# Attention and MoE on one core: PSUM banks and copies of the first two batches rearranged, last output chunk stored in two column halves

## Chip, cores, metric

One core of one Trainium2 chip. The metric is the device time of one execution in microseconds (us); all times below are us. Times inside a profile count from the start of its span, and the span is some 2 us shorter than the execution's time.

## The reference

```python
B, H, S, D = 8, 8, 576, 64; pool = 8; Sp = 72
k_p = k.reshape(B, H, Sp, pool, D).mean(axis=3); v_p = the same of v
attn = softmax(q @ k_p^T / sqrt(D))
x = (attn @ v_p).transpose(0, 2, 1, 3).reshape(4608, 512)
h = x @ w_in                    # 512 -> 2048
out = (h * cos(h)) @ w_out      # 2048 -> 512, fp32
```

## The kernel before

The 4608 tokens are worked in nine tiles of 512. Tile `t` has an up stage (eight blocks of eight 128x512 matmuls into `banks[fp % 3]`, ScalarE's cosine, VectorE's multiply) and a down stage (64 matmuls). The attention of batch `t + 1` is threaded into the down stage of tile `t`. Batch 0 runs alone at the start. Batches 0 and 1 pool k and v and transpose q on TensorE; from batch 2 on, POOL (GpSimd) pools and SP issues DMA transposes of q and of the pooled k. In profiles PE is TensorE, DVE VectorE, ACT ScalarE. `us` are the four units of a batch (256 tokens by four heads), REST its last 64 tokens, S their scores and V their values; `kpz` is the pooled k, `kz` the same transposed, `qT` the transposed q; half clock means that a 128x512 matmul takes 0.43 instead of 0.216. The parts that the argument touches, with cuts marked `...`:

```python
def put_kz(b, ps, pj0, pj1, copies):            # pooled k out of PSUM, four copies
    for a in range(2):
        for r in range(2):
            copies[r](out=dst[half[r], pj0:pj1, a, r, 0:Sp], in_=ps[half[a]])
...
# start, batch 0 ("mixed" = VectorE, ScalarE in turn on one PSUM tile)
q_transpose_mm(0, qbanks, 0, mixed)             # qbanks: two halves of banks[2]
...
pool_k_mm(0, obanks[1], 2, 4, vec2)
warm_up(2, obanks[0])
q_transpose_mm(0, qbanks, 1, vec2)
sums_first(0, us[0], obanks[0])                 # the sums, Ln and Exp(-1) of unit 0
sums_first(0, us[1], obanks[1])
...
# up stage of tile 0, after block 5 and block 6
pool_k_mm(1, obanks[0], 0, 4, mixed)
q_transpose_mm(1, obanks[::-1], 0, mixed_r)
...
# down stage: (number of matmuls before, what is put in)
fill = [(1, REST scores), (4, S 0), (8, REST values), (8, pool_v_mm), (8, S 1), (8, V 0), (16, S 2),
        (16, V 1), (24, S 3), (24, V 2), (36, V 3)]          # tile 0, shortened
...
if 0 < t and b + 1 < B:                          # b = t + 1
    load_kv(b + 1, "k", k); ...; load_kv(b + 1, "v", v)      # POOL's queue
...
if b + 1 < B:
    pool_add(b + 1, "k"); pool_add(b + 1, "v")               # POOL
```

The softmax here doesn't subtract the row's maximum and nothing guards it: scores larger than these inputs give would overflow.

Of the kernel before, what the change touches and what calls it, by code (L numbers as in the profile page):

```python
# [10 lines left out]
BF16 = mybir.dt.bfloat16  # L11
# [3 lines left out]
POOL = 8  # L15
# [4 lines left out]
def kernel(  # L20
# [9 lines left out]
    nc = tc.nc  # L30
    B, H, S, D = q.shape
    Sp = S // POOL
# [51 lines left out]
    def load_even(dst, b, src, j0=0, j1=KCH):  # L84
        nc.gpsimd.dma_start(out=dst[:, j0:j1].rearrange("p j t d -> p j (t d)"), in_=even_view(src, b, j0, j1))
# [36 lines left out]
    def v_part(b):  # L122
        return vz[b % 2][:, :, 0:4:3, :]

    def put_kz(b, ps, pj0, pj1, copies):
        dst = kz[b % 2].rearrange("p (j a r) n -> p j a r n", a=2, r=2)
        for a in range(2):
            for r in range(2):
                copies[r](out=dst[half[r], pj0:pj1, a, r, 0:Sp], in_=ps[half[a]])

    def pool_add(b, which):

# [11 lines left out]
            s = s.rearrange("p (j a) t d -> p j a t d", a=2)  # L144
            add(out=v_part(b), in0=s[..., 0, :], in1=s[..., 1, :], op=ADD)  # L145

    def pool_k_mm(b, bank, pj0, pj1, copies):

        kb = staged["k", b]
        ps = bank[:, 0:(pj1 - pj0) * Sp].rearrange("p (j n) -> p j n", n=Sp)  # L150
        for pj in range(pj0, pj1):
            for t in range(ROW):
                for rows in half:
                    nc.tensor.matmul(ps[rows, pj - pj0, :], lhsT=kb[rows, pj, t, :], rhs=groups[rows, t, :],
                                     start=(t == 0), stop=(t == ROW - 1))
        put_kz(b, ps, pj0, pj1, copies)

    def pool_v_mm(b, pair):
        vb = staged["v", b]
# [16 lines left out]
    def q_flat(b):  # L176
        return staged["q", b].rearrange("p j t d -> p (j t d)")
# [2 lines left out]
        qT_tile(b)  # L180
        nc.sync.dma_start_transpose(out=att["qT", b], in_=q_flat(b))

    def q_transpose_mm(b, banks_, j, copies):

        if ("qT", b) not in att:
            qT_tile(b)
        for bank, g0, g1, copy in zip(banks_, (9 * j, 9 * j + 5), (9 * j + 5, 9 * j + 9), copies):
            ps = bank.bitcast(BF16)[:, 0:(g1 - g0) * 128].rearrange("p (g n) -> p g n", n=128)
            for g in range(g0, g1):
                nc.tensor.matmul(ps[:, g - g0, :], q_flat(b)[:, g * 128:(g + 1) * 128], identity, is_transpose=True)  # L190
            copy(out=att["qT", b][:, g0:g1, :], in_=ps)

    def scores(b, u, pair):
        (c0, n), (h0, nh) = u
# [54 lines left out]
        att["inv", b, u] = inv  # L249

    def values_then(b, u, ao):
        (c0, n), (h0, nh) = u
        ex = att.pop(("ex", b, u))
        for i in range(nh):
            pj, hp = divmod(h0 + i, 2)
            nc.tensor.matmul(ao[hp * 64:hp * 64 + 64, (i // 2) * n:(i // 2 + 1) * n],
                             lhsT=vz[b % 2][:, pj, 3 * hp, :], rhs=ex[:, i * n:(i + 1) * n])
        nc.vector.tensor_mul(out=x_out(b, u, slice(0, 128)), in0=cols(ao, u), in1=cols(att.pop(("inv", b, u)), u))
# [8 lines left out]
    def up_mm(t, fp, k0=0, k1=KCH):  # L267

        h = banks[fp % 3]
        for j in range(2):  # L270
            fc = 2 * fp + j
            for ki in range(k0, k1):
                nc.tensor.matmul(h[:, j, :], lhsT=w_in_sb[fc // 4][:, ki, (fc % 4) * 128:(fc % 4 + 1) * 128],  # L273
                                 rhs=xT[:, ki, t * TILE:(t + 1) * TILE],
                                 start=(ki == 0), stop=(ki == KCH - 1))

    def up_g(t, fp):
        h = banks[fp % 3]
        cos = msb.tile([128, 2, TILE], FP32, name="cos", tag="cos", bufs=2)
        nc.scalar.activation(out=cos, in_=h, func=ACTF.Sin, bias=half_pi[:, :1])  # L280
        nc.vector.tensor_mul(out=g_sb[:, 2 * fp:2 * fp + 2, :], in0=h, in1=cos)  # L281

    def down_mm(o, ms, fc):
        nc.tensor.matmul(o, lhsT=g_sb[:, fc, ms * 128:(ms + 1) * 128],  # L284
                         rhs=w_out_sb[fc // 4][:, fc % 4, :], start=(fc == 0), stop=(fc == FFCH - 1))

    def down_out(t, ms, ps):
        o = msb.tile([128, d_model], FP32, name="o_sb", tag="o_sb")
        nc.vector.tensor_copy(out=o, in_=ps)  # L289
        rows_of = out.rearrange("(b p t) m -> b t p m", b=B, t=ROW)  # L290
        for i, rows in enumerate(half):
            b_, pos = divmod((t * TILE + ms * 128) // 64 + i, ROW)
            nc.sync.dma_start(out=rows_of[b_, ORDER[pos]], in_=o[rows])


    EX = 5
# [43 lines left out]
    load_even(staged["q", 1], 1, q, 2, 4)  # L340
    load_w_out(0)
    load_even(staged["v", 1], 1, v)
    for cg in range(1, 4):
        load_w_out(cg)

    def warm_up(n, bank):

        for i in range(n):
            nc.tensor.matmul(bank, lhsT=warm[:, 0:128], rhs=warm)

    vec2 = (nc.vector.tensor_copy,) * 2
    mixed = (nc.vector.tensor_copy, nc.scalar.copy)
    mixed_r = mixed[::-1]
    qbanks = [banks[2][:, 0, :], banks[2][:, 1, :]]
    us = BY_HEADS

    warm_up(10, obanks[0])
    pool_k_mm(0, obanks[1], 0, 2, mixed)
    warm_up(2, obanks[0])
    q_transpose_mm(0, qbanks, 0, mixed)  # L360
    warm_up(2, obanks[0])
    scores(0, us[0], banks[0])
    scores(0, us[1], banks[1])
    pool_k_mm(0, obanks[1], 2, 4, vec2)
    warm_up(2, obanks[0])
    q_transpose_mm(0, qbanks, 1, vec2)
    sums_first(0, us[0], obanks[0])
    sums_first(0, us[1], obanks[1])
    scores(0, us[2], banks[0])
    scores(0, us[3], banks[1])  # L370
    nc.vector.memset(kz[1], 0.0)
    pool_v_mm(0, banks[2])
    sums_first(0, us[2], obanks[0])
    sums_first(0, us[3], obanks[1])
    values_then(0, us[0], obanks[0])
    values_then(0, us[1], obanks[1])
    nc.vector.memset(vz[1], float(POOL))
    values_then(0, us[2], obanks[0])
    values_then(0, us[3], obanks[1])
    sin_tables()  # L380

    for t in range(NT):
        b = t + 1
        if t == 0:
            for fp in range(2):
                up_mm(t, fp, 0, 2)
        for fp in range(FFCH // 2):
            up_mm(t, fp, 2 if t == 0 and fp < 2 else 0)
            up_g(t, fp)
            if t == 0:  # L390
                if fp == 5:
                    pool_k_mm(1, obanks[0], 0, 4, mixed)
                    q_transpose_mm(1, obanks[::-1], 0, mixed_r)
                elif fp == 6:
                    q_transpose_mm(1, obanks[::-1], 1, mixed)
            elif b < B:
                if fp == 0:
                    q_transpose(b)
                elif fp == 2:
                    k_transpose(b)  # L400
        mms = [(ms, fc) for ms in range(4) for fc in range(FFCH)]
        if t == 0:
            mms = [(ms, fc) for hm in range(2) for cg in range(4) for ms in range(2 * hm, 2 * hm + 2)
                   for fc in range(4 * cg, 4 * cg + 4)]


        def S_(n, bank):
            return lambda: scores(b, us[n], banks[bank])

        def V_(n, bank):  # L410
            return lambda: values(b, us[n], banks[bank])

        fill = []
        if t < B:
            exp_tables()
            fill = [(1, lambda: scores(t, REST, banks[2])), (8 if t == 0 else 12, lambda: values(t, REST, banks[1]))]
        if t == 0:
            fill[1:1] = [(4, S_(0, 0))]
            fill += [(8, lambda: pool_v_mm(1, banks[2])), (8, S_(1, 0)), (8, V_(0, 2)), (16, S_(2, 0)), (16, V_(1, 1)),
                     (24, S_(3, 0)), (24, V_(2, 2)), (36, V_(3, 1))]  # L420
        elif b < B:
            us = BY_TOKENS
            fill[1:1] = [(5, S_(0, 0))]
            fill += [(15, S_(1, 2)), (18, V_(0, 0)), (25, S_(2, 2)), (28, V_(1, 1)), (35, S_(3, 2)), (38, V_(2, 0)),
                     (46, V_(3, 1))]
        if 0 < t and b + 1 < B:
            load_kv(b + 1, "k", k)
            q_tile(b + 1)
            load_even(staged["q", b + 1], b + 1, q)
            load_kv(b + 1, "v", v)  # L430
        fi = 0
        for n, (ms, fc) in enumerate(mms):
            while fi < len(fill) and fill[fi][0] <= n:
                fill[fi][1]()
                fi += 1
            down_mm(obanks[ms % 2], ms, fc)
            if fc == FFCH - 1:
                down_out(t, ms, obanks[ms % 2])
        if t < B:
            sin_tables()  # L440
        if t == 0:
            load_kv(2, "k", k)
            q_tile(2)
            load_even(staged["q", 2], 2, q)
            load_kv(2, "v", v)
            for i in range(2):
                nc.gpsimd.memset(kpz[i], 0.0)  # L447
        if b + 1 < B:
            pool_add(b + 1, "k")
            pool_add(b + 1, "v")  # L450
# [1 line left out]
_INS = ['q', 'k', 'v', 'moe_w_in', 'moe_w_out']  # L452
_OUTS = [((4608, 512), 'float32')]
# [25 lines left out]
```

## Time and profile before

| quantity | before |
|---|---|
| time, median of the runs beside the changed kernel | 332.41 (331.54 to 332.8) |
| span of the profiled run | 329.6 |
| TensorE (PE) busy | 303.3 (92%) |
| tile 0 up, from the start of the first up matmul to the first down matmul | 22.19 to 43.96 |
| tile 0 down, to the first up matmul of tile 1 | 43.96 to 70.79 |
| tile 1; tile 2 | 39.4; 31.65 |
| end of PE's work to end of span | 4.8 |

A row of the table is a stretch between two starts in the timeline of PE. A steady tile takes 31.65, so whatever is above this is a hole or a lowered clock. Lines from the page, the chain of work, the waits and the timeline are in the prediction. Here is one view that it uses but does not show, the queue of SP (start, duration of the issue, what):

```profile
75.34 8.35 SPq L181 DMA_TRANSPOSE qT<-q_b  x1
83.80 5.40 SPq L168 DMA_TRANSPOSE kz<-kpz  x1
...
113.17 2.82 SPq L181 DMA_TRANSPOSE qT<-q_b  x1
116.08 1.36 SPq L168 DMA_TRANSPOSE kz<-kpz  x1
```

The first pair belongs to tile 1 and stands among POOL's loads (issued at 70.2 to 72.7, landed by 88.9). The second, in tile 2, comes when the last of its loads lands (113.3).

### The profile page before, as it was taken

The page shows a single profiled execution, that of the slowest core. Times are in us where ns is not written, and L with a number is a line of the kernel's source. Part 1 is how long each engine was busy: PE and PEld are TensorE (multiplying, and loading weights), DVE is VectorE, ACT ScalarE, POOL GpSimd, SP SyncE. Part 2 cuts the span into 40 slices and gives each one's busy share as a digit, 9 for nine tenths or more (in the row PEclk, how much of TensorE's full clock was granted, in tenths as well). Part 3 has the DMA queues.
Part 4 walks back from the last instruction along what each step waited for, and adds up shares of the span by engine and source line. Part 5 has one row for each costly group of instructions (what it writes and reads, how often), then busy time and mean ns, then how long its engine had stood idle before and what let it go on. Part 6 is the DMA issues. An engine that isn't in the chain of part 4 may idle for free.

```text
span 329.6 us, 4548 instructions
## 1 busy us (share of the span) xinstructions
PE 303.3 (92%) x1784; PEld 153.4 (47%) x1784; DVE 172.1 (52%) x209; ACT 206.2 (63%) x253; POOL 131.0 (40%) x88
## 2 busy tenths in 40 slices
PE   6769698699499999999999999999999999999994
PEld 2524354344245446544654555456445544444441
DVE  5345433437415574567466647564665556525721
ACT  2566385546549569956994797579668966704500
POOL 8422009983892974395449445931000000000000
PEclk9979897999969999999999999999999999999999
DMA  7999995139909951993299249901290130041032
GB/s 102 188 207 206 207 174 75 33 60 194 171 2 154 212 89 10 178 215 55 29 195 198 35 54 203 187 15 32 47 162 0 33 82 16 2 91 37 0 67 64
DMA packets 47686, 33.60 MB, mean 102 GB/s; under 512 B 25904, under 2 KB 43056, under 8 KB 47664
## 3 DMA queue, kind: packets, MB, share of 16 engines
q0 software_dynamic: 20016, 18.36, 36.3%
q1 hardware_dynamic: 27648, 14.95, 22.5%
q8 instruction: 14, 0.23, 0.3%
q14 instruction: 8, 0.07, 0.1%
HBM read 36.70 MB, written 9.44 MB: 140 GB/s over the span
## 4 chain that ended last, share of the span: by engine, by line
PE 77%; POOL 8%; DMA 6%; ACT 4%; issue 2%; DVE 1%; POOLq 0%; DVEq 0%; ACTq 0%
PE bank L273 34%; PE obank L284 33%; PE bank L199 4%; PE bank L225 4%; POOL kv_st L138 4%; DMA kv_st<-in_k_dram 3%; DMA kz<-kpz 2%; POOL kv_st L139 2%; DMA q_b<-in_q_dram 2%; POOL kpz L447 1%; ACT cos L280 1%; ACT ex L203 1%; ACT L261 1%; POOL kpz L142 1%; ACT lnc L247 1%
## 5 line engine op out<-in xcount | busy, mean ns | idle before, releaser
L284 PE MATMUL obank<-w_out_sb,g_sb 128*128 128x512 bf16 x576 | 140.3, 385 | 3.2 <-DVE o_sb L289 3.2
L273 PE MATMUL bank<-xT,w_in_sb 128*128 128x512 bf16 x576 | 129.0, 385 | 0.0
L280 ACT ACTIVATE cos<-bank,half_pi 128x1024 f32<-128x1024 f32 x72 | 80.2, 1115 | 73.8 <-PE bank L273 73.8
L281 DVE TENSOR_TENSOR g_sb<-bank,cos 128x1024 bf16<-128x1024 f32 x72 | 88.1, 1224 | 55.2 <-ACT cos L280 55.2
L273 PEld LDWEIGHTS <-w_in_sb 128*128 128x128 bf16 x576 | 56.8, 99 | 69.6 <-issue 3.8
L284 PEld LDWEIGHTS <-g_sb 128*128 128x128 bf16 x576 | 56.0, 99 | 58.0 <-issue 6.2
L234 DVE TENSOR_TENSOR xT<-bank,inv 64x512 bf16<-64x512 f32 (+1 forms) x72 | 45.3, 629 | 66.1 <-ACT inv L232 64.0
L138 POOL TENSOR_TENSOR kv_st<-kv_st 72x2048 f32<-72x2048 bf16 x12 | 48.7, 4061 | 32.6 <-DMA kv_st<-in_k_dram 31.9
L231 ACT ACTIVATE lnc<-bank 64x512 f32<-64x512 f32 (+1 forms) x72 | 39.2, 544 | 11.6 <-PE bank L225 9.8
L203 ACT ACTIVATE ex<-bank 72x1024 bf16<-72x1024 f32 (+1 forms) x40 | 36.3, 927 | 7.3 <-PE bank L199 7.2
L289 DVE COPY o_sb<-obank 128x512 f32<-128x512 f32 x36 | 24.2, 689 | 19.0 <-PE obank L284 18.4
L139 POOL TENSOR_TENSOR kv_st<-kv_st 72x1024 f32<-72x1024 f32 x12 | 28.2, 2348 | 1.0
L199 PE MATMUL bank<-qT,kz 128*72 128x256 bf16 (+1 forms) x192 | 23.5, 254 | 5.2 <-DMA kz<-kpz 5.2
L199 PEld LDWEIGHTS <-kz 128*72 128x72 bf16 x192 | 17.9, 117 | 14.5 <-DMA kz<-kpz 5.6
L225 PE MATMUL bank<-ex,vz 72*128 72x256 bf16 (+1 forms) x176 | 20.3, 246 | 2.7 <-DVE vz L164 1.7
L232 ACT ACTIVATE inv<-lnc 128x512 f32<-128x512 f32 (+1 forms) x36 | 21.0, 582 | 1.1
L225 PEld LDWEIGHTS <-vz 72*128 72x128 bf16 x176 | 14.1, 100 | 12.2 <-DVE vz L164 2.0
L145 POOL TENSOR_TENSOR vz<-kv_st 72x512 bf16<-72x512 f32 x6 | 7.6, 1264 | 25.3 <-PE bank L225 24.7
L142 POOL TENSOR_TENSOR kpz<-kv_st 72x512 bf16<-72x512 f32 x12 | 15.0, 1267 | 0.5
L104 POOL DMA_DIRECT2D kv_st<-in_v_dram x6 | 5.0, 841 | 18.9 <-PE bank L162 18.9
L261 ACT ACT_TABLE_LOAD x9 | 11.5, 1283 | 0.9 <-PEq L463 0.7
L264 ACT ACT_TABLE_LOAD x9 | 11.5, 1283 | 0.2
(48 smaller groups left out, 77.7 us busy)
## 6 DMA issues: line engine op xcount, KB each, us to landing
out_dram<-o_sb SPq DMA_DIRECT2D x72, 128.0 KB, 2.7
kv_st<-in_v_dram POOLq DMA_DIRECT2D x8, 576.0 KB, 14.8
kv_st<-in_k_dram POOLq DMA_DIRECT2D x7, 576.0 KB, 8.9
q_b<-in_q_dram POOLq DMA_DIRECT2D x6, 576.0 KB, 11.4
w_in_sb<-in_moe_w_in_dram POOLq DMA_DIRECT2D x4, 512.0 KB, 13.6
w_out_sb<-in_moe_w_out_dram POOLq DMA_DIRECT2D x4, 512.0 KB, 18.5
q_b<-in_q_dram POOLq DMA_DIRECT2D x4, 288.0 KB, 12.2
kv_st<-in_k_dram POOLq DMA_DIRECT2D x2, 288.0 KB, 5.0
```

The source lines that it names most:

```text
L138: add(out=s, in0=x[:, :, 0:4, :], in1=x[:, :, 4:8, :], op=ADD)
L139: add(out=s[:, :, 0:2, :], in0=s[:, :, 0:2, :], in1=s[:, :, 2:4, :], op=ADD)
L199: nc.tensor.matmul(flat[:Sp, i * n:(i + 1) * n].rearrange("p (g n) -> p g n", n=64), lhsT=kz[b % 2][:, 2 * (h0 + i) + r, 0:Sp], rhs=att["q ...
L203: nc.scalar.activation(out=ex[:, 0:nh * n], in_=flat[:Sp, 0:nh * n], func=ACTF.Exp, scale=scale / POOL)
L225: nc.tensor.matmul(pair[:, hp, (i // 2) * n:(i // 2 + 1) * n], lhsT=vz[b % 2][:, pj, 2 * hp:2 * hp + 2, :].rearrange("p a d -> p (a d)"), ...
L231: nc.scalar.activation(out=lnc[half[1 - hp]], in_=pair[half[1 - hp], hp, 0:w], func=ACTF.Ln)
L234: nc.vector.tensor_mul(out=x_out(b, u, half[hp]), in0=cols(pair[half[hp], hp, :], u), in1=cols(inv[half[1 - hp]], u))
L273: nc.tensor.matmul(h[:, j, :], lhsT=w_in_sb[fc // 4][:, ki, (fc % 4) * 128:(fc % 4 + 1) * 128], rhs=xT[:, ki, t * TILE:(t + 1) * TILE], st ...
L280: nc.scalar.activation(out=cos, in_=h, func=ACTF.Sin, bias=half_pi[:, :1])
L281: nc.vector.tensor_mul(out=g_sb[:, 2 * fp:2 * fp + 2, :], in0=h, in1=cos)
L284: nc.tensor.matmul(o, lhsT=g_sb[:, fc, ms * 128:(ms + 1) * 128], rhs=w_out_sb[fc // 4][:, fc % 4, :], start=(fc == 0), stop=(fc == FFCH - 1))
L289: nc.vector.tensor_copy(out=o, in_=ps)
```

## The change

The intent: no two engines on one PSUM tile in the first two batches, so that nobody takes turns; the inverse of each unit made as soon as its sums are there; the down stage of tile 0 in an order in which each bank is free when it is wanted; and a shorter end. The diff, cut to its core:

```diff
-def put_kz(b, ps, pj0, pj1, copies):      # copies[r](...)
+def put_kz(b, ps, pj0, pj1, copy):        # copy(...): one engine
     # pool_k_mm and q_transpose_mm now return a function that takes the copy; q_transpose_mm fills one bank
 # start
-    q_transpose_mm(0, qbanks, 0, mixed)
+    puts = q_transpose_mm(0, banks[2][:, 0, :], 0, 5), q_transpose_mm(0, obanks[0], 5, 9)
+    puts[0](vec)
+    puts[1](act)
 ...
-    warm_up(2, obanks[0])
-    q_transpose_mm(0, qbanks, 1, vec2)
-    sums_first(0, us[0], obanks[0])
+    sums_first(0, us[0], banks[0][:, 0, :])
+    puts = q_transpose_mm(0, banks[2][:, 0, :], 9, 14), q_transpose_mm(0, obanks[0], 14, 18)
+    puts[0](vec)
+    puts[1](act)
 ...  # sums and values of units 2 and 3 likewise in tiles of their own
 # up stage of tile 0: blocks 4 to 6, ScalarE's copy between cosine and multiply
+                if fp == 4:
+                    puts = pool_k_mm(1, obanks[0], 0, 2), pool_k_mm(1, obanks[1], 2, 4)
+                elif fp in (5, 6):
+                    puts = q_transpose_mm(1, obanks[0], g0, g0 + 5), q_transpose_mm(1, obanks[1], g0 + 5, g0 + 9)
+                puts[0](vec)
+                between = ((puts[1], act),)
+            up_g(t, fp, between)
 # down stage of tile 0, shortened
+            (1, REST scores), (2, S 0), (4, pool_v_mm), (8, REST values), (8, S 1), (8, V 0), (14, S 2),
+            (16, V 1), (22, S 3), (32, V 2), (40, V 3)
 # the memsets of kpz go from behind the load of v for batch 2 to the start
 # the last 128 rows
+    def last_chunk():
+        for hc in range(2):
+            ... 16 matmuls of 256 columns into banks[hc]
+            down_out(t, ms, ps, hc * 256, (nc.sync, nc.scalar))
```

More of the change, by code (lines that the diff above doesn't have):

```diff
@@ L128, in put_kz @@
             for r in range(2):
-                copies[r](out=dst[half[r], pj0:pj1, a, r, 0:Sp], in_=ps[half[a]])
+                copy(out=dst[half[r], pj0:pj1, a, r, 0:Sp], in_=ps[half[a]])
     def pool_add(b, which):
@@ L145, in pool_add, with pool_k_mm @@
             add(out=v_part(b), in0=s[..., 0, :], in1=s[..., 1, :], op=ADD)
-    def pool_k_mm(b, bank, pj0, pj1, copies):
+    def pool_k_mm(b, bank, pj0, pj1):
         kb = staged["k", b]
@@ L155, in pool_k_mm @@
                                      start=(t == 0), stop=(t == ROW - 1))
-        put_kz(b, ps, pj0, pj1, copies)
+        return lambda copy: put_kz(b, ps, pj0, pj1, copy)
     def pool_v_mm(b, pair):
@@ L181, in q_transpose, with q_transpose_mm @@
         nc.sync.dma_start_transpose(out=att["qT", b], in_=q_flat(b))
-    def q_transpose_mm(b, banks_, j, copies):
+    def q_transpose_mm(b, bank, g0, g1):
         if ("qT", b) not in att:
             qT_tile(b)
-        for bank, g0, g1, copy in zip(banks_, (9 * j, 9 * j + 5), (9 * j + 5, 9 * j + 9), copies):
-            ps = bank.bitcast(BF16)[:, 0:(g1 - g0) * 128].rearrange("p (g n) -> p g n", n=128)
-            for g in range(g0, g1):
-                nc.tensor.matmul(ps[:, g - g0, :], q_flat(b)[:, g * 128:(g + 1) * 128], identity, is_transpose=True)
-            copy(out=att["qT", b][:, g0:g1, :], in_=ps)
+        ps = bank.bitcast(BF16)[:, 0:(g1 - g0) * 128].rearrange("p (g n) -> p g n", n=128)
+        for g in range(g0, g1):
+            nc.tensor.matmul(ps[:, g - g0, :], q_flat(b)[:, g * 128:(g + 1) * 128], identity, is_transpose=True)
+        return lambda copy: copy(out=att["qT", b][:, g0:g1, :], in_=ps)
     def scores(b, u, pair):
@@ L275, in up_mm, with up_g @@
                                  start=(ki == 0), stop=(ki == KCH - 1))
-    def up_g(t, fp):
+    def up_g(t, fp, between=()):
         h = banks[fp % 3]
@@ L280, in up_g @@
         nc.scalar.activation(out=cos, in_=h, func=ACTF.Sin, bias=half_pi[:, :1])
+        for put, copy in between:
+            put(copy)
         nc.vector.tensor_mul(out=g_sb[:, 2 * fp:2 * fp + 2, :], in0=h, in1=cos)
@@ L285, in down_mm, with down_out @@
                          rhs=w_out_sb[fc // 4][:, fc % 4, :], start=(fc == 0), stop=(fc == FFCH - 1))
-    def down_out(t, ms, ps):
+    def down_out(t, ms, ps, c0=0, queues=(nc.sync, nc.sync)):
         o = msb.tile([128, d_model], FP32, name="o_sb", tag="o_sb")
-        nc.vector.tensor_copy(out=o, in_=ps)
+        n = ps.shape[1]
+        nc.vector.tensor_copy(out=o[:, 0:n], in_=ps)
         rows_of = out.rearrange("(b p t) m -> b t p m", b=B, t=ROW)
@@ L292, in down_out @@
             b_, pos = divmod((t * TILE + ms * 128) // 64 + i, ROW)
-            nc.sync.dma_start(out=rows_of[b_, ORDER[pos]], in_=o[rows])
+            queues[i].dma_start(out=rows_of[b_, ORDER[pos], :, c0:c0 + n], in_=o[rows, 0:n])
+    def last_chunk():
+        t, ms = NT - 1, 3
+        for hc in range(2):
+            ps = banks[hc][:, 0, 0:256]
+            for fc in range(FFCH):
+                nc.tensor.matmul(ps, lhsT=g_sb[:, fc, ms * 128:(ms + 1) * 128],
+                                 rhs=w_out_sb[fc // 4][:, fc % 4, hc * 256:(hc + 1) * 256],
+                                 start=(fc == 0), stop=(fc == FFCH - 1))
+            down_out(t, ms, ps, hc * 256, (nc.sync, nc.scalar))
     EX = 5
@@ L342 @@
     load_even(staged["v", 1], 1, v)
+    for i in range(2):
+        nc.gpsimd.memset(kpz[i], 0.0)
     for cg in range(1, 4):
@@ L349, in warm_up @@
             nc.tensor.matmul(bank, lhsT=warm[:, 0:128], rhs=warm)
-    vec2 = (nc.vector.tensor_copy,) * 2
-    mixed = (nc.vector.tensor_copy, nc.scalar.copy)
-    mixed_r = mixed[::-1]
-    qbanks = [banks[2][:, 0, :], banks[2][:, 1, :]]
+    vec, act = nc.vector.tensor_copy, nc.scalar.copy
     us = BY_HEADS
     warm_up(10, obanks[0])
-    pool_k_mm(0, obanks[1], 0, 2, mixed)
-    warm_up(2, obanks[0])
-    q_transpose_mm(0, qbanks, 0, mixed)
-    warm_up(2, obanks[0])
+    pool_k_mm(0, obanks[1], 0, 2)(vec)
+    warm_up(2, banks[1][:, 0, :])
+    puts = q_transpose_mm(0, banks[2][:, 0, :], 0, 5), q_transpose_mm(0, obanks[0], 5, 9)
+    puts[0](vec)
+    puts[1](act)
+    warm_up(2, banks[1][:, 0, :])
     scores(0, us[0], banks[0])
     scores(0, us[1], banks[1])
-    pool_k_mm(0, obanks[1], 2, 4, vec2)
-    warm_up(2, obanks[0])
-    q_transpose_mm(0, qbanks, 1, vec2)
-    sums_first(0, us[0], obanks[0])
+    pool_k_mm(0, obanks[1], 2, 4)(vec)
+    sums_first(0, us[0], banks[0][:, 0, :])
+    puts = q_transpose_mm(0, banks[2][:, 0, :], 9, 14), q_transpose_mm(0, obanks[0], 14, 18)
+    puts[0](vec)
+    puts[1](act)
     sums_first(0, us[1], obanks[1])
     scores(0, us[2], banks[0])
-    scores(0, us[3], banks[1])
+    scores(0, us[3], banks[2])
     nc.vector.memset(kz[1], 0.0)
-    pool_v_mm(0, banks[2])
+    nc.vector.memset(vz[1], float(POOL))
+    pool_v_mm(0, banks[1])
     sums_first(0, us[2], obanks[0])
-    sums_first(0, us[3], obanks[1])
-    values_then(0, us[0], obanks[0])
-    values_then(0, us[1], obanks[1])
-    nc.vector.memset(vz[1], float(POOL))
-    values_then(0, us[2], obanks[0])
-    values_then(0, us[3], obanks[1])
+    values_then(0, us[0], obanks[1])
+    values_then(0, us[1], banks[1][:, 0, :])
+    sums_first(0, us[3], banks[2][:, 0, :])
+    values_then(0, us[2], obanks[1])
+    values_then(0, us[3], obanks[0])
+    up_mm(0, 0, 0, 2)
+    up_mm(0, 1, 0, 2)
     sin_tables()
@@ L383 @@
         b = t + 1
-        if t == 0:
-            for fp in range(2):
-                up_mm(t, fp, 0, 2)
         for fp in range(FFCH // 2):
             up_mm(t, fp, 2 if t == 0 and fp < 2 else 0)
-            up_g(t, fp)
+            between = ()
             if t == 0:
-                if fp == 5:
-                    pool_k_mm(1, obanks[0], 0, 4, mixed)
-                    q_transpose_mm(1, obanks[::-1], 0, mixed_r)
-                elif fp == 6:
-                    q_transpose_mm(1, obanks[::-1], 1, mixed)
-            elif b < B:
+                if fp == 4:
+                    puts = pool_k_mm(1, obanks[0], 0, 2), pool_k_mm(1, obanks[1], 2, 4)
+                elif fp in (5, 6):
+                    g0 = 9 * (fp - 5)
+                    puts = q_transpose_mm(1, obanks[0], g0, g0 + 5), q_transpose_mm(1, obanks[1], g0 + 5, g0 + 9)
+                if fp in (4, 5, 6):
+                    puts[0](vec)
+                    between = ((puts[1], act),)
+            up_g(t, fp, between)
+            if 0 < t and b < B:
                 if fp == 0:
@@ L415 @@
             exp_tables()
-            fill = [(1, lambda: scores(t, REST, banks[2])), (8 if t == 0 else 12, lambda: values(t, REST, banks[1]))]
+            fill = [(1, lambda: scores(t, REST, banks[2])), (12, lambda: values(t, REST, banks[1]))]
         if t == 0:
-            fill[1:1] = [(4, S_(0, 0))]
-            fill += [(8, lambda: pool_v_mm(1, banks[2])), (8, S_(1, 0)), (8, V_(0, 2)), (16, S_(2, 0)), (16, V_(1, 1)),
-                     (24, S_(3, 0)), (24, V_(2, 2)), (36, V_(3, 1))]
+            fill[1:] = [(2, S_(0, 0)), (4, lambda: pool_v_mm(1, banks[1])), (8, lambda: values(t, REST, banks[2])),
+                        (8, S_(1, 0)), (8, V_(0, 1)), (14, S_(2, 2)), (16, V_(1, 0)), (22, S_(3, 1)), (32, V_(2, 2)),
+                        (40, V_(3, 0))]
         elif b < B:
@@ L431 @@
         fi = 0
+        if t == NT - 1:
+            mms = mms[:-FFCH]
         for n, (ms, fc) in enumerate(mms):
@@ L445 @@
             load_kv(2, "v", v)
-            for i in range(2):
-                nc.gpsimd.memset(kpz[i], 0.0)
         if b + 1 < B:
@@ L450 @@
             pool_add(b + 1, "v")
+    last_chunk()
 _INS = ['q', 'k', 'v', 'moe_w_in', 'moe_w_out']
```

## The prediction

> **What bounds the kernel now.** I read the page first, for the bound of the whole and where it is not kept. Units are us, times count from the span's start.
>
> ```profile
> PE 303.3 (92%) x1784; PEld 153.4 (47%) x1784; DVE 172.1 (52%) x209; ACT 206.2 (63%) x253; POOL 131.0 (40%) x88
> ...
> PE   6769698699499999999999999999999999999994
> ...
> PEclk9979897999969999999999999999999999999999
> ```
>
> TensorE is the bound, but its holes and its lowered clocks lie in the first 12 slices (8.24 us each) and in the last. From there on it is full. The chain of work, in order of time, gives the length of an undisturbed tile of 512 tokens:
>
> ```profile
> 110.39 13.81 PE bank L273 x64
> ...
> 142.03 13.81 PE bank L273 x64
> ...
> 173.68 13.81 PE bank L273 x64
> ```
>
> So a steady tile takes 31.65. Tile 1 started at 70.79 (the timeline of PE), so it took 39.6, which is 7.95 too long. What comes before 70.79 is the part that the change rewrites. The waits of PE name the holes:
>
> ```profile
> PE bank L199 <- DMA kz<-kpz: 5.2, 1, 5.2
> PE obank L284 <- DVE o_sb L289: 3.2, 1, 3.2
> PE obank L190 <- ACT kz L129: 2.5, 1, 2.5
> PE obank L243 <- ACT ex L203: 1.7, 2, 1.2
> PE bank L190 <- DVE qT L191: 1.7, 2, 1.1
> PE bank L225 <- DVE vz L164: 1.7, 1, 1.7
> ```
>
> The first is in tile 1, the second and sixth in the down stage of tile 0, the third in its up stage, the others in the start. The timeline of PE shows that a hole costs more than itself:
>
> ```profile
> 38.10 0.45 PE L190 MATMUL obank<-identity,q_b 128*128 128x128 bf16 x4 [2.49 <-ACT kz L129]
> 38.34 3.55 PE L273 MATMUL bank<-xT,w_in_sb 128*128 128x512 bf16 x8
> ```
>
> Eight matmuls take 3.4 here and 1.73 (8 x 0.216) in a steady tile: half the clock, some 1.6 lost. After the 5.2 hole, and after the 1.7 one at 51.06, it is the same.
>
> **What the Trainium skill says.** "TensorE: Matmul & The Clock Gate", Part 1, says that the clock falls to half after an idle window of about 3.4 us and comes back after a busy one, with a window that runs free. The trace agrees (3.4 against 1.73), though here holes of 1.7 and 2.5 in sparse work were enough. "PSUM — Partial Sum Buffer", section on PSUM bank collisions, says that two engines must not touch one bank and quadrant at once, so accesses must be ordered by bank. The trace agrees with such an order: at L129 VectorE and ScalarE take turns on one tile (36.27 DVE, 36.74 ACT, 37.16 DVE, 37.66 ACT), and PE waits for the last. "Trainium Kernel Development and Optimization", Key Constraints, says that the DMAs of SP, ACT and POOL share 16 DMA engines, so that a second queue saves only issue time. The trace agrees for the sharing: beside the loads of 70 to 89 the transposes of tile 1 took 14.7 and 7.4 to land, and in tile 2 4.8 and 3.8.
>
> **The change, part by part.** I walked the new order of instructions by hand with the old durations.
>
> Start (before: up stage from 22.25). The q transposes of a half go to two tiles, so the second four need not wait for the copy of the first five: scores 0.6 earlier. The Ln and Exp of unit 0 come before the second q half, which lands at 11.8 (issue 4.80 plus 7.0) in both kernels. In the chain of before, ScalarE ran without a pause from 14.16:
>
> ```profile
> 14.16 0.61 ACT lnc L247
> ...
> 14.79 0.64 ACT inv L248
> ...
> 15.45 0.61 ACT lnc L247
> ...
> 16.08 0.63 ACT inv L248
> 16.71 1.42 ACT ex L203 x2
> ```
>
> Now the first pair runs at about 11.6 to 12.8. One q copy comes to ScalarE (0.59), and the last inverse ends near 19.2 instead of 21.0. The first up matmuls need only units 0 and 1, whose values now lie in tiles of their own and are multiplied by 18.4, once the v load (14.6) has been pooled and copied. Up starts at 18.5: **3.7 gained**. All weights are there (the first w_in lands at 17.2, the third at 22.2).
>
> Up of tile 0 (before 22.25 to 43.96, 21.7). Work is 64 x 0.216 = 13.8, k pooling 1.4, transposes 1.65: 16.9. The copies go to VectorE before its multiply (4 x 0.31 or 0.49) and to ScalarE after its cosine (4 x 0.27 or 0.6), each on its own bank, with a whole block of eight matmuls (1.73) before the bank is wanted. So the 2.5 hole and the half clock after it go. I leave 1.5 for the half clock at its start, since the start stays sparse: 18.4, **3.3 gained**, ending at 36.9. k1 (25.1), q1 (30.6), w_in 3 (29.0) and the first w_out (33.0) have landed when wanted.
>
> Down of tile 0 (before 43.96 to 70.79, 26.8). Matmuls 13.8; four scores and four values at 0.44 each, v pooling 1.1, the two small ones 0.5: 18.9. Walking the order leaves three waits: v pooling on the multiply of the last up block, 1.0; the last scores on a values bank, 0.7; the third output row on the copy of the first, 0.5. That is 21.2 with small gaps, no half clock: **5.6 gained**. Tile 1 starts at about 58.2, not 70.8.
>
> Tile 1. The POOL chain moves less. The kpz memsets (3.56) leave it, but k2 lands only at 47.6, behind a full DMA, so the k sums start at 47.6, not 53.5, and the loads for batch 3 go out at 64.3, not 70.2. The transposes of batch 2 go out at about 60.5, ahead of those loads. The 5.2 wait and the half clock after it vanish: **7.95 gained**.
>
> Tile 2. The same collision comes back here. POOL needs 26.9 from loads to loads (70.23 to 97.11), so the loads for batch 4 start near 90.2, and tile 2 starts at 58.2 + 31.65 = 89.8; its transposes go out 2.7 later, into those loads. Before, with loads 0.6 ahead of the tile, kz landed 20.4 after its start and was wanted after 15.2. With two fewer stores in the way I take 19: wait 4, half clock 2: **6 lost**. Tile 3 is then clear of it.
>
> End. The last two lines of the timeline's outputs:
>
> ```profile
> 321.37 0.69 DVE L289 COPY o_sb<-obank 128x512 f32<-128x512 f32 x1 [2.76 <-PE obank L284]
> 324.82 0.69 DVE L289 COPY o_sb<-obank 128x512 f32<-128x512 f32 x1 [2.76 <-PE obank L284]
> ```
>
> From the end of PE's work 4.8 pass. The half-width copy should take about 0.42 (0.27 less, an estimate from 0.69), and two stores issued side by side save one issue of 0.62. The 32 half matmuls cost as much as 16 (0.11 each, as in the scores): **0.9 gained**.
>
> Sum: 3.7 + 3.3 + 5.6 + 7.95 - 6 + 0.9 = 15.45, and 332.6 - 15.45 = **317**.
>
> **Rivals.** (a) The collision does not come back: POOL's loads slip 3 late or more and the transposes pass ahead of them. Then about 311. Against it: each tile POOL gains only 31.65 - 26.9 = 4.75 on PE, so it must pass through the bad zone, about as wide, at some tile. (b) It comes back in full, twice, or the gain before tile 1 is swallowed: the DMA is full up to 46 whatever PE does, so a faster PE only meets later loads. If all of the gain of the first two parts is lost in waits for loads, 324. For it: DMA at 9 tenths in every early slice; against it: by the landing times every load has over 2 to spare. But this also bounds me from the other side: if PE is 3 slower than I think, tile 2 waits that much less. (c) The longer list of VectorE and ScalarE work in up blocks 4 to 6 becomes the bound: 1.23 + 1.26 on VectorE and 1.11 + 1.1 on ScalarE against 1.73 + 1.4 of PE in block 4; it fits, and a miss costs 1. (d) Only the end matters and the rest hides: 331. Nothing in the chain of work, which is PE nearly throughout, speaks for it.
>
> **Range and chances.** Half clock comes by windows that I can't place (each 1.5 to 2), and the collision is between 0 and 8. I take 311 to 323. Under 2% needs more than 326, that is over half of the sum failing: 0.04 for same, 0.01 for slower.
>
> **What would show it.** In the changed profile: the first long L273 block at 18 to 19.5 (the start); no wait for the kz copies over 0.5 (up); down of tile 0 at 21 to 22.5 and no wait for o_sb over 1; no wait for the kz transposes in tile 1 and one of 2 to 6 in tile 2 with matmuls at half clock behind it; the last stores landing about 4 after PE's end. The prediction is wrong if PE waits for w_in or w_out, if tile 1 still waits for kz, or if the collision is seen nowhere.

## The result

| | before | after |
|---|---|---|
| time, median | 332.41 | 318.67 (316.8 to 325.31, 4 runs) |
| ratio | | 0.9572 (0.9519 to 0.9624) |
| profiled span | 329.6 | 316.3 |

The profiled runs and all runs compared here are fast ones; the changed kernel's run of 325.31 counts as slow and is left out. A ratio here is the mean time of one kernel's fast runs over that of the other's of the same rounds, so not quite the ratio of the medians.

The slow runs here need not be a state of the chip. Two were profiled, and in both the time lies in waits of the kernel itself: after_memback waits 13.9 for kz, and ag_whole2q begins its up stage at 21.37 behind a 1.6 wait for v, with 18.4 for the stage where after_gate takes 16.2. Of the 13 runs of the three kernels that meet the collision in tile 2 (the changed one, after_memback, after_warm) four were slow, of the 22 of the gated change two. The run of 325.31 was not profiled; if it is a long wait for kz, the ratio leaves out a part of what the change costs.

Stage by stage, from the timelines of PE of the two profiled runs:

| stretch | before | after | gained | predicted |
|---|---|---|---|---|
| start (first up matmul) | 22.19 | 20.10 | 2.1 | 3.7 |
| tile 0 up | 21.8 | 16.2 | 5.5 | 3.3 |
| tile 0 down | 26.8 | 21.4 | 5.45 | 5.6 |
| tile 1 | 39.4 | 31.6 | 7.8 | 7.95 |
| tile 2 | 31.65 | 40.2 | -8.5 | -6 |
| end, with the half matmuls | | | 0.95 | 0.9 |
| sum | | | 13.3 | 15.45 |

The page of the changed kernel (busy us and share; busy tenths in 40 slices of 7.9 us; granted clock in tenths):

```profile
PE 297.4 (94%) x1766; PEld 154.0 (49%) x1798; DVE 173.3 (55%) x213; ACT 205.7 (65%) x254; POOL 130.9 (41%) x88
...
PE   7789899999999299999999999999999999999995
...
PEclk9799999999999879999999999999999999999999
```

The holes of slices 3 to 12 are gone, and there is one new one in slice 14, with a lowered clock behind it. The waits of PE (total, times, longest):

```profile
PE bank L198 <- DMA kz<-kpz: 6.4, 1, 6.4
PE bank L189 <- DMA q_b<-in_q_dram: 1.9, 1, 1.9
...
PE bank L162 <- DVE g_sb L283: 0.9, 1, 0.9
PE bank L198 <- DVE xT L233: 0.5, 1, 0.5
```

Of the waits before, only that for kz is left at size, and the timeline of PE shows that it now lies in tile 2 (start, duration, what; in brackets the idle time before):

```profile
103.67 1.03 PE L286 MATMUL obank<-w_out_sb,g_sb 128*128 128x512 bf16 x4
111.05 1.07 PE L198 MATMUL bank<-qT,kz 128*72 128x256 bf16 x4 [6.35 <-DMA kz<-kpz]
111.91 3.19 PE L286 MATMUL obank<-w_out_sb,g_sb 128*128 128x512 bf16 x7
```

Seven matmuls took 2.98 to the next start (114.89 less 111.91; 0.43 each) where a steady tile has 1.51. The queues of SP and of POOL show why kz came late:

```profile
61.32 2.90 SPq L181 DMA_TRANSPOSE qT<-q_b  x1
64.33 1.36 SPq L168 DMA_TRANSPOSE kz<-kpz  x1
...
92.31 10.76 SPq L181 DMA_TRANSPOSE qT<-q_b  x1
103.16 5.37 SPq L168 DMA_TRANSPOSE kz<-kpz  x1
```

```profile
80.91 2.49 POOL L142 TENSOR_TENSOR kpz<-kv_st 72x512 bf16<-72x512 f32 x2
...
91.15 0.84 POOL L104 DMA_DIRECT2D kv_st<-in_k_dram  x1
```

The first pair (tile 1) went out before POOL's loads of 65.3 and landed after 4.9 and 3.9. The second (tile 2) went out 1.2 after the first of the next loads, which POOL's queue began at 91.15; qT took 17.8 to land and kz 7.8. The pooled k itself had been ready since 83.4 (the timeline of POOL), so POOL's sums were not what it waited for. In the six collisions looked at (tile 1 before, tile 2 here and in before_early, after_memback and after_warm, tile 3 in after_early) kz landed 0.5 to 4.1 after the last of the three loads, that of v: here at 111.0, v at 108.9.

### The profile page after: what moved, and what is told of

Same layout as the page of the kernel before. It is cut to its first block, busy times and chain, and to the rows that moved or that the text cites. A ratio compares the mean times of both kernels' runs of the same rounds, so it can differ in the third digit from the quotient of the medians.

```text
span 316.3 us, 4555 instructions
## 1 busy us (share of the span) xinstructions
PE 297.4 (94%) x1766; PEld 154.0 (49%) x1798; DVE 173.3 (55%) x213; ACT 205.7 (65%) x254; POOL 130.9 (41%) x88
## 4 chain that ended last, share of the span: by engine, by line
PE 65%; DMA 15%; POOL 11%; ACT 2%; issue 1%; DVE 1%; POOLq 0%; ACTq 0%; DVEq 0%
PE obank L286 29%; PE bank L273 28%; DMA kv_st<-in_k_dram 12%; POOL kv_st L138 6%; PE bank L224 3%; PE bank L198 3%; POOL kv_st L139 3%; DMA kz<-kpz 2%; POOL kpz L142 2%; PE bank L304 1%; ACT ex L202 1%; ACT L261 0%; ACT cos L280 0%; PE obank L256 0%; POOL vz L145 0%
## 5 line engine op out<-in xcount | busy, mean ns | idle before, releaser
L286 PE MATMUL obank<-w_out_sb,g_sb 128*128 128x512 bf16 x542 | 133.1, 382 | 1.1 <-DVE o_sb L292 0.3
L273 PE MATMUL bank<-xT,w_in_sb 128*128 128x512 bf16 x563 | 125.5, 379 | 0.6
L273 PEld LDWEIGHTS <-w_in_sb 128*128 128x128 bf16 x576 | 56.1, 98 | 67.3 <-issue 0.4
L286 PEld LDWEIGHTS <-g_sb 128*128 128x128 bf16 x560 | 54.1, 98 | 52.1 <-issue 2.0
L292 DVE COPY o_sb<-obank 128x512 f32<-128x512 f32 x35 | 23.5, 689 | 15.4 <-PE obank L286 14.8
L224 PE MATMUL bank<-ex,vz 72*128 72x256 bf16 (+1 forms) x176 | 20.1, 244 | 0.3 <-ACT ex L202 0.2
## 6 DMA issues: line engine op xcount, KB each, us to landing
w_out_sb<-in_moe_w_out_dram POOLq DMA_DIRECT2D x4, 512.0 KB, 18.3
```

What stands on the lines that cost most here:

```text
L224: nc.tensor.matmul(pair[:, hp, (i // 2) * n:(i // 2 + 1) * n], lhsT=vz[b % 2][:, pj, 2 * hp:2 * hp + 2, :].rearrange("p a d -> p (a d)"), ...
L273: nc.tensor.matmul(h[:, j, :], lhsT=w_in_sb[fc // 4][:, ki, (fc % 4) * 128:(fc % 4 + 1) * 128], rhs=xT[:, ki, t * TILE:(t + 1) * TILE], st ...
L286: nc.tensor.matmul(o, lhsT=g_sb[:, fc, ms * 128:(ms + 1) * 128], rhs=w_out_sb[fc // 4][:, fc % 4, :], start=(fc == 0), stop=(fc == FFCH - 1))
L292: nc.vector.tensor_copy(out=o[:, 0:n], in_=ps)
```

## Experiments

Each kernel ran beside the kernel before on the same chip; "ratio" is that to the kernel before. "Gate" below means the tiny copy of experiment 2. None gives a wrong result. The runs of experiment 4 are from chip 8, those of the other experiments from chip 11.

**1. after_early and before_early: the transposes issued earlier.**

```diff
-                if fp == 0: q_transpose(b)
-                elif fp == 2: k_transpose(b)
 # in the down stage
+            if n == 36 and b + 1 < B:
+                ...                      # tile 0: the loads of batch 2, moved up with it
+                pool_add(b + 1, "k"); pool_add(b + 1, "v")
+                q_transpose(b + 1); k_transpose(b + 1)
```

> The changed kernel, with the transposes of q and k of batch t+2 issued in the down stage of tile t, ahead of its last two rows of stores, and so ahead of the loads for the next batch; nothing else moves. Theory A (the wait for kz in tile 2 is a collision of the transposes with the loads on the shared DMA engines): the wait of 6.35 us and the half clock after it (about 2.1) go, 318.2 - 8.4 = about 310 us, no wait of PE for kz anywhere. Rival B (the pooled k itself is late, so POOL's chain sets it): the wait stays, 316 to 319. Rival C (the collision only moves to another tile): a wait for kz in tile 3 or later, 314 to 318.

The edit moves POOL's sums (and the loads of batch 2) up in the program with the transposes, as the cut shows, so "nothing else moves" is not exact; their order on POOL's queue stays.

Measured: 317.12 (ratio 0.9588). Theory A's number failed, rival C held. There is no wait in tile 2; in tile 3 PE waits 6.6 for kz. The chain of work of this run names its cause (start, duration, what):

```profile
115.45 8.88 DMA kv_st<-in_k_dram
...
124.81 16.38 DMA kz<-kpz
141.19 0.04 issue
141.23 1.07 PE bank L198 x4
```

The transposes of tile 3's batch were issued at 115.79, POOL's loads at 115.45: moving the transposes by a part of a tile met the next loads, since POOL goes from loads to loads in 26.5 (88.97 to 115.45) while PE takes 31.65. The collision moved, it did not go.

> The kernel before, with the same move of the transposes. Theory A: the 5.2 us wait in tile 1 and the half clock behind it go, 332.4 - 7.95 = about 324.5 us, so the change's other parts are worth the same with and without the collision (after_early about 14 below before_early). Rival B: no change, 331 to 333.

Measured: 324.11 (ratio 0.9794, 0.9737 to 0.9852, unclear at 2%), near theory A's number, and no wait of PE for kz. Against the 331.01 of the same rounds it is 6.9 less; the wait and its half clock are 7.8 in the profile. The transposes of tile 1's batch were issued from 65.07 and landed after 5.1 and 3.7, the loads came at 70.95. The next pair did meet loads (those were issued at 96.4 and after; qT took 14.3 to land, kz 7.4). But its kz landed at 116.4, and tile 2, which starts at 103.33, asks for it 15.2 later, at 118.5: the same collision, hidden.

**2. after_gate: the loads held back behind the transposes.**

```diff
         if 0 < t and b + 1 < B:
+            nc.gpsimd.tensor_copy(out=token, in_=kz[b % 2][0:1, 0, 0:1])
             load_kv(b + 1, "k", k)
```

> The changed kernel, with one tiny copy on POOL that reads the transposed k of the tile, ahead of the loads for the next batch, so that the loads go out after the transposes in every tile. Theory A: the transposes land in about 5 us in all tiles, no wait of PE for kz, about 310.5 us, although the loads and all of POOL's sums come later. Rival B (POOL's chain sets the end): later loads make it slower, above 320 us.

Measured: 307.77 (307.32 to 308.93), ratio 0.931 (0.9253 to 0.9366): below every other kernel. The transposes of tile 2 were issued in 2.06 and 1.38 and landed in 4.3 and 3.7:

```profile
90.56 2.06 SPq L181 DMA_TRANSPOSE qT<-q_b  x1
92.71 1.38 SPq L168 DMA_TRANSPOSE kz<-kpz  x1
```

Tiles 1 to 6 take 31.65 each (the chain of work has its blocks of 64 up matmuls at 56.13, 87.77, 119.42, 151.07 and so on to 246.01). Rival B falls: the loads for batch 4 went out 5.5 later (96.7 against 91.2) and nothing waited for POOL. By the medians this is 10.9 below the changed kernel, but the two ran in different rounds; by the ratios to the kernel before (0.931 against 0.9572) it is 2.6% of 332, so 8.7, which is what the tile 2 of the profile had lost (8.5). The profiles say the same: their spans differ by 10.3, of which 8.5 is tile 2 and 1.75 the start, which was late in the changed kernel's profiled run.

**3. after_memback: is the move of the memsets worth something?** The two memsets of kpz put back behind the load of v for batch 2.

> The changed kernel with the memsets of kpz back in their old place, behind the load of v for batch 2. My theory: no change (318 to 319, within 0.5), because POOL idles 7.2 us before 48.4, waiting for k of batch 2 to land behind a full DMA, and the memsets (3.56) now fit into that hole. Rival: the memsets are on POOL's chain and every later load comes 3.6 later, which moves the collision of tile 2 by that much: 3 to 6 us faster, or the same amount slower.

Measured: 317.92 (ratio 0.9592), the same as the changed kernel. In its timeline the memsets end at 43.2 and POOL then idles 5.4 until k lands. Its profile fell in a slow run (a wait for kz of 13.9 in tile 2), so only this order of events, and the wait itself, are read from it. The move costs and gives nothing here.

**4. The parts, each alone, on the gated kernel before.** The gate takes away the collision, which would otherwise hide or add some 8 in any part. The base:

> The kernel before, with the same tiny copy on POOL ahead of the loads of batch 3 and later (loads after the transposes). Base for the parts. Theory A: 324 us, as the early transposes gave (332.4 - 7.95 = 324.4), no wait for kz. If the gate does more than take the collision away (the changed kernel gained 10.9 by it, not 8.4), it is below 322.

Measured: 325.51 (323.33 to 327.58), ratio 0.9803 (0.9743 to 0.9864, unclear at 2%). No wait for kz. The gate does here what the early transposes did, within the noise of this kernel.

> The gated kernel before plus the start of the change alone (banks, copies and one inverse at once of batch 0; old up stage, old down order, old end, memsets in the old place). My theory: the up stage begins at 18.4 instead of 22.25 when q lands before 8, so 3.7 less: 320.3. Rival: the start only meets a full DMA earlier and PE waits later for weights or k: under 2 less, 322 or more, with a wait of PE for w_in or k.

Measured: 319.02, ratio 0.961, 6.5 below the base's median. In the profiles the up stage begins 3.6 earlier (19.15 against 22.75), as predicted; but it is also 1.8 shorter (20.6 against 22.4 to the first down matmul), since the half clock at its beginning is mostly gone. PE waits for no weights.

> The gated kernel before plus the up stage of the change alone (pooled k of batch 1 in two banks, one engine to a bank, between cosine and multiply). My theory: the 2.5 wait for the copies of kz and the half clock after it (1.6) go: 4 less, 320. Rival: only the wait goes and the half clock comes elsewhere: 2.5 less, 321.5.

Measured: 319.72, ratio 0.9614, 5.8 below the base. In the profiles the up stage shortens from 22.4 to 17.75, so 4.65; the down stage, which this edit doesn't touch, is also 1.7 shorter (25.1 against 26.8), since the base ran part of it at half clock behind a wait of 3.15 for o_sb and this run did not. In the timeline of PE nothing stands between the up blocks and the transposes, and all run at full clock (columns as above):

```profile
34.68 1.90 PE L273 MATMUL bank<-xT,w_in_sb 128*128 128x512 bf16 x7
36.41 0.67 PE L189 MATMUL obank<-identity,q_b 128*128 128x128 bf16 x9
36.92 1.89 PE L273 MATMUL bank<-xT,w_in_sb 128*128 128x512 bf16 x8
```

Those lines answer to the two of the kernel before in the prediction, with its 2.49 wait and its eight matmuls in 3.55. The edit gives each engine its own bank, but it also pools one block earlier, so that a whole block of matmuls lies before the bank's next use. Which of the two took the wait away is not separated.

> The gated kernel before plus the new order and banks of tile 0's down stage alone. My theory: 26.8 becomes 21.3, so 5.5 less: 318.5, with no wait for the stores' copy over 0.5. Rival: the order was not the limit but ScalarE's chain, which is as long as before: the waits reappear as waits for ex or xT, under 3 less, 321 or more.

Measured: 318.56, ratio 0.96, 6.95 below the base. In the profiles the down stage is 21.4 (44.86 to 66.30) against 26.8 (45.15 to 71.97). The waits left in it are the three that the prediction had walked:

```profile
PE bank L162 <- DVE g_sb L283: 0.9, 1, 0.9
PE bank L198 <- DVE xT L233: 0.5, 1, 0.5
PE obank L286 <- DVE o_sb L292: 0.3, 1, 0.3
```

The three parts together are 19.2 by the medians, and the gated change without its tail is 16.6 below the base (308.91 against 325.51, but on another chip; 15.2 by the ratios). The profiles explain the difference: tile 1 begins at 71.97 in the base, at 66.53, 65.95 and 66.30 with the parts, so 5.4, 6.0 and 5.7 earlier, and at 55.96 in after_gate, 16.0 earlier. Without the 1.7 that g_up gained outside of its stage the parts add up to 15.4, so they hardly overlap. The rest of the 19.2 is within the scatter of the base's median (its runs span 4).

**5. The end.** The gated change with the last chunk whole and one queue; in halves and one queue; whole and two queues.

```diff
-            down_out(t, ms, ps, hc * 256, (nc.sync, nc.scalar))
+            down_out(t, ms, ps, hc * 256, (nc.sync, nc.sync))      # ag_oneq
```

> The changed kernel with the gate, its last chunk whole again and on one queue. By the profiles so far the end of the span comes 4.78 after PE's end with a whole chunk and 3.75 with the change, and the half matmuls cost 0.06 more: 0.95 slower than with it (307.8), so about 308.7; from PE's end to the span's end 4.8. Rival: the end hides nothing else and the gain is noise: 307.8.

> The changed kernel with the gate, last chunk in two column halves, but both stores on SP. By my sum the halves are worth 0.27 (the copy) and the second queue 0.62 (one issue): from PE's end to the span's end 4.4, about 308.4. Rival: the second queue is worth nothing, since all queues share the DMA engines: 3.8.

> The changed kernel with the gate, last chunk whole, its two stores on SP and ScalarE's queue. From PE's end to the span's end 4.15 by my sum (4.78 - 0.62). Rival as for the other: 4.8.

| last chunk | time | ratio | PE's end to span's end |
|---|---|---|---|
| whole, one queue (ag_notail) | 308.91 | 0.9343 | 4.7 |
| whole, two queues (ag_whole2q) | 308.74 | 0.9334 | 4.6 (profile of a slow run) |
| halves, one queue (ag_oneq) | 308.18 | 0.9319 | 4.1 |
| halves, two queues (after_gate, other rounds) | 307.77 | 0.931 | 3.8 |

The sum of 0.95 held, its split did not: the halves are worth 0.6 and the second queue 0.3 beside them, 0.2 alone. That agrees with the Trainium skill, "Trainium Kernel Development and Optimization", Key Constraints, which says that issuing from a second queue saves only issue time: it is less than the 0.62 of one issue. By the ratios the intervals of these four overlap, so the order rests on the profiles' ends. They read (start, duration, what) in the changed kernel:

```profile
310.76 0.42 DVE L292 COPY o_sb<-bank 128x256 f32<-128x256 f32 x1 [1.05 <-PE bank L304]
311.22 2.24 ACTq L296 DMA_DIRECT2D out_dram<-o_sb  x2
312.51 0.42 DVE L292 COPY o_sb<-bank 128x256 f32<-128x256 f32 x1 [1.32 <-PE bank L304]
```

The copy is 0.42 as estimated, and the first half's copy and stores lie beside the second half's matmuls.

**6. after_warm: is the half clock a cost of the wait?**

```diff
+        if t == 2:
+            fill[1:1] = [(5, lambda: warm_up(24, banks[0][:, 0, :]))]
```

> The changed kernel without the gate; in tile 2, ahead of the scores that wait for kz, 24 idle matmuls (5.2 us at full clock) into the bank of these scores, so TensorE is busy during the wait. The wait stays on the clock of the DMA. If the half clock is a second cost of the wait, the matmuls behind it take 0.216 each, not 0.43, and the time is 2 below that of the changed kernel with the same wait (318.7 to 316.5). Rival: the slow matmuls have another cause: they stay at 0.43, and the time is as before. The wait differs from run to run, so the verdict is to be read from the matmuls behind it.

Measured: 321.53 (316.15 to 326.43; ratio 0.9593). The times scatter (two of the four runs are slow) and say nothing. The timeline of PE in a fast run does:

```profile
102.86 5.34 PE L365 MATMUL bank<-warm 128*128 128x512 bf16 x24
111.12 0.63 PE L198 MATMUL bank<-qT,kz 128*72 128x256 bf16 x4 [2.91 <-DMA kz<-kpz]
111.58 1.67 PE L286 MATMUL obank<-w_out_sb,g_sb 128*128 128x512 bf16 x7
```

kz came at the same moment (111.1), the wait was filled but for 2.91, and the same seven matmuls took 1.51 to the next start, not 2.98. So the half clock follows from TensorE's idleness (one trace each; tile 2 took 39.9 here, of which 8.3 were filled or waited, so nothing came on top), and cost about 2 on top of the wait in the changed kernel: 1.47 on these seven, 0.40 on the scores before them (0.86 against 0.46 to the next start) and 0.09 on the values behind.

## Why the prediction was right, and where it was off

- **Total.** 317 predicted, 318.67 measured, inside 311 to 323. That it came so near is in part luck: in the profiles the start gained 1.6 less than forecast, the up stage 2.2 more, and tile 2 lost 2.5 more. The first two cancel, so tile 1 began at 57.72 for the 58.2 forecast.
- **Signs.** Two of the forecast signs fell outside their ranges: the first up matmul (20.1 for 18 to 19.5) and the wait in tile 2 (6.35 for 2 to 6). The others held.
- **Slips in the working.** 7.95 takes one start from the chain of work (110.39) and one from the timeline (70.79); by the timeline alone it is 7.8. Behind the 1.71 hole it is not "the same": eight matmuls took 2.98 there, not 3.4. And 64.3 + 26.9 is 91.2, not 90.2; the loads did go out at 91.15.
- **Start.** Mis-sized in the compared profile: up began at 20.1, not 18.5. There the first load of q let the transposes start at 9.01 (7.83 before), and the eight scores behind them ran at half clock (1.84 for 1.15). In six profiles with this start the transposes began at 7.5 to 8.2 and up at 18.3 to 18.5, which is the step as predicted; in g_start up began at 19.15 and in the slow run of ag_whole2q at 21.37, both behind waits for loads (v 0.7 and 1.6). So the step depends on when q and v land. The change leaves the order of these loads as it was; what sets their landing is not shown.
- **Up.** Right in its mechanism, mis-sized: the 1.5 left for half clock at its start did not come, since the start became denser (g_start shows 1.8 of this by itself), so 16.2 for 18.4.
- **Down.** Right, 21.4 for 21.2, with the waits 0.9, 0.5 and 0.3 for 1.0, 0.7 and 0.5.
- **Tile 1.** Right: no wait, 31.6.
- **Tile 2.** The mechanism was right, and it is shown, not argued: the wait goes when the loads are held behind the transposes (after_gate) and moves to tile 3 when the transposes are moved (after_early). That the two meet at the DMA engines, and not for instance at the memory, no run separates. The size was off: I took kz to land 19 after the tile's start, it was 21.7 (111.05 less 89.36), so the wait was 6.35 for 4, and the loss 8.5 for 6. The slip above is a part of it: the loads went out 1.8 after the tile's start (91.15 against 89.36), not 0.4, and kz lands behind the last of them. The transposes of q alone took 10.76 to issue, more than the 8.35 before.
- **End.** The sum is right, the split between halves and queue was not (experiment 5).
- **Rivals.** (a), no collision, came true only in the gated kernel: the changed kernel with it would have been below my 311, so rival (a) was sized too small by about 3, mainly since the up stage was 2.2 shorter than forecast (16.2 for 18.4). Of (b), the collision did come back in full, but once: it cost 8.5 in tile 2, where it had cost 7.8 in tile 1; of waits for loads only those of q and v at the start are seen, none for weights. (c), VectorE and ScalarE as the bound, is seen nowhere. (d) is out.

What stays open: why the wait for kz differs so much from run to run (6.35 here, 13.9 in one slow run of after_memback). The loads were late with it: v took 16.1 to land here and 25.0 there, and kz landed 2.1 and 0.5 after it. What slowed the loads is not shown.

## What to carry to other kernels

When a stage at the front gets faster, look at the queues that run at their own pace: here POOL's loads, which gain 5 us a tile on TensorE, met the DMA transposes one tile later than before and took back 8.5 of some 22 us. A collision of two streams of different periods is not cured by shifting one of them once; tie one to the other (one tiny copy that reads what must have landed), which was worth some 8.7 us here. Order small work such that the bank it wants has been free for a whole block of matmuls. One reading engine to a PSUM tile came with this here, and its own share is not shown.

## What the Trainium skill lacked or had wrong

- "TensorE: Matmul & The Clock Gate", Part 1, gives an idle window of about 3.4 us before half clock. Here a hole of 2.49 in sparse work was followed by slow matmuls in all five traces that have it (eight in 2.4 to 3.4 for 1.73), one of 1.71 only in the kernel before (eight in 2.98, in four other traces 1.73), and one of 2.91 behind busy work not at all (after_warm). The page could say that holes shorter than the window can be enough when the work around them is sparse.
- "DMA: Bandwidth & Descriptors", in its table of rules, says that a transpose beside ordinary DMAs needs nothing. That is said of correctness; in time, qT took 17.8 to land beside three loads and 4.9 alone, and its issue held SP's queue for 10.76 instead of 2.9, so that kz could not even be issued. We found no figure for this on the page.
- "PSUM — Partial Sum Buffer", on bank collisions, orders two engines on a bank but gives no price. Four copies of pooled k taking turns between two engines held TensorE for 2.49; in g_up, with one engine to a bank and a block of matmuls more before the bank's next use, nothing was held. The turns were taken also where the two engines read different halves of the rows (36.74 ScalarE on rows 0 to 63, 37.16 VectorE on rows 64 to 127), which the page's rule by bank and quadrant would let run together.
